# A chunked linear-attention kernel with a gated low-rank layer: decay carried over pairs of chunks, r*k packed into 384 columns, copies shared between ScalarE and VectorE, unread matrix products at the start, and a new hand order

## The chip, the cores and the metric

The kernel runs on one core of a Trainium2 chip. The metric is device time in microseconds for one launch; a time given for "the runs" is the median of several. The profile comes from one further execution. Its engines are called PE (TensorE), DVE (VectorE), ACT (ScalarE), POOL (GpSimd) and SP (SyncE, which here only issues DMAs).

## The reference

Two stages are computed. The first is a linear attention with a decaying state, for batch 4, 8 heads, 768 steps and head dimension 48:

```
for t in range(S):
    cur = einsum('bhd,bhe->bhde', u * k_t, v_t)
    y_t = einsum('bhd,bhde->bhe', r_t, state + cur)
    state = w_t[..., None] * state + einsum('bhd,bhe->bhde', k_t, v_t)
```

The second takes each of the 3072 tokens as a row x of 384 numbers and adds a mixture of low-rank terms: `logits = x @ w_gate` for 8 experts of rank 16, the two largest are kept and normalised by a softmax, and the result is `x + sum_e weight_e * (x @ A[e]) @ B[e]`.

## The kernel before, in words

The 768 steps of a batch are cut into 6 chunks of L = 128 steps, so there are NT = 24 chunks, numbered 0 to 23 across the four batches. A chunk is also one tile of 128 tokens for the second stage. Heads lie in P = 4 pairs; a pair takes 128 partitions, 48 rows for each head and 16 rows of zeros behind them.

Work on chunk t is cut into small stages, each a function of `tile_kernel` with the chunk's number as its argument. A text ORDER (lines 32 to 76) lists all stages of all chunks, and the program issues them exactly so under a manual schedule: an engine's queue is the order in which its stages appear there. Nothing reorders them later, so an instruction that waits holds up everything behind it on its engine.

The stages of the first part, with their engines:
- `load_w`, `load_rk`, `consts` (lines 132 to 160) issue DMAs on SP: w for one or two chunks, r and k of a chunk transposed (512 KB, into a ring of 10 tiles), and the constants u (`ub_f`), A with w_gate (`aw_f`) and B (`b_f`). `load_v` (line 150) issues on POOL's queue: 1, 2 and 3 chunks for the first batch, then all 6 chunks of a batch at once. `castc` (line 162) turns the constants to bf16 on POOL.
- `ln` (ACT) takes log w; `cs` (PE, line 183) sums it over the chunk by a product with a triangle of ones, into `x_ps`; `expp` and `expm` (ACT, lines 189 and 194) give exp of the sums (`ep`, a ring of three tiles) and of their negatives.
- `qmul` (POOL, line 198) is r*k over 512 columns; `rmul` (POOL, line 203) is r times `ep`; `kmul` (DVE, line 208) is k times the negative exponential.
- `dgmm` (PE, line 225) sums r*u*k over each head, by four products, into the bank `kd`; `dv` (DVE, line 238) multiplies v by it. `ktr` (PE, line 218) transposes k into the same bank and `ktev` (ACT, line 230) copies it out as `ks`.
- `amm` (PE, line 244) makes the chunk's scores `a_ps`; `aev` (DVE, line 252) masks them. `kv` (PE, line 258) adds the chunk to the state `s_ps`, which stays in PSUM; `resc` (DVE, line 267) multiplies the state by the chunk's whole decay, after each of the first five chunks of a batch; `sev` (ACT, line 272) copies it out as `sb`.
- `ymd`, `ymS`, `ymv` (PE, lines 277 to 296) add the three parts of y in `y_ps`, and `yev` (ACT, line 298) copies it out as `xT`.

The second part works on gates of three tiles (at the end one of two, and one of one): `zl` (PE, line 309) makes `z_ps`; `top`, `gsel`, `gnorm`, `zw` (DVE), `gexp` (ACT), and `gmul` and `gmul2` (POOL) choose and weigh; `zT` (PE) and `zTev` (DVE, line 378) transpose. Then for each tile `dmm` (PE, line 385), `oev` (ACT, line 394) and `store` (a DMA on SP, line 399).

PSUM is full: `x_ps`, `y_ps`, `kd` and `s_ps` have one buffer each, `a_ps` one of two banks, and `z_ps`, `zT_ps` and `d_ps` share two. So the next chunk's `cs` waits until `kmul` has read `x_ps`, the next `amm` until `aev` has read `a_ps`.

Of the kernel before, what the change touches and what calls it, by code (L numbers as in the profile page):

```python
# [36 lines left out]
ktr.2 ktev.2 cs.4 expp.4 expm.4 ymd.2 load_rk.7 kv.2 resc.2 sev.2 qmul.3 dgmm.3 dv.3 load_v.6 ymS.2 ymv.2
yev.2 rmul.3 amm.3 ktr.3 ktev.3 load_rk.8 kmul.4 cs.5 expp.5 expm.5 aev.3 castc.1 zl.2 top.2 gexp.2 ln.6
kv.3 resc.3 sev.3 gsel.2 ymd.3 ymS.3 qmul.4 dgmm.4 ymv.3 yev.3 rmul.4 amm.4 kmul.5 cs.6 load_w.10 dv.4 ktr.4
ymd.4 ymS.4 gmul.2 gnorm.2 rmul.5 aev.4 ymv.4 load_rk.9 gmul2.2 zw.2 expp.6 expm.6 kmul.6 ktev.4 kv.4 resc.4  # L40
ln.8 load_rk.10 load_rk.11 zT.2 zTev.2 yev.4 sev.4 qmul.5 dgmm.5 dv.5 cs.7 expp.7 expm.7 amm.5 aev.5 kmul.7
castc.2 dmm.0 dmm.1 oev.1 store.1 ymd.5 ymS.5 rmul.6 amm.6 aev.6 ymv.5 cs.8 oev.0 store.0 dmm.2 qmul.6
dgmm.6 dv.6 yev.5 zl.5 top.5 gsel.5 expp.8 expm.8 ktr.6 ktev.6 kmul.8 gexp.5 oev.2 store.2 ymd.6 ymv.6 yev.6
kv.6 resc.6 sev.6 qmul.7 dgmm.7 rmul.7 amm.7 load_w.12 cs.9 expp.9 expm.9 gmul.5 gnorm.5 load_rk.13 dv.7
ktr.7 ymd.7 ktev.7 ymS.7 kv.7 load_rk.12 load_w.14 ln.10 aev.7 ymv.7 yev.7 qmul.8 dgmm.8 gmul2.5 zw.5 zT.5
kmul.9 cs.10 resc.7 sev.7 expp.10 expm.10 rmul.8 amm.8 load_v.12 dv.8 ktr.8 ymd.8 ktev.8 zTev.5 dmm.3 dmm.4
oev.3 oev.4 store.3 ymS.8 kv.8 rmul.9 aev.8 ymv.8 yev.8 kmul.10 resc.8 sev.8 qmul.9 dgmm.9 dv.9 load_rk.14
qmul.10 rmul.10 amm.9 aev.9 cs.11 expp.11 expm.11 rmul.11 zl.8 top.8 gsel.8 ktr.9 ktev.9 kmul.11 gexp.8
gmul.8 ln.12 ymd.9 ymS.9 ymv.9 yev.9 kv.9 resc.9 sev.9 qmul.11 dgmm.10 dv.10 gnorm.8 gmul2.8 amm.10 aev.10
load_w.16 cs.12 expp.12 rmul.12 qmul.12 store.4 ktr.10 ktev.10 load_rk.16 load_rk.15 zw.8 expm.12 kmul.12  # L50
dmm.5 oev.5 store.5 load_rk.17 ln.14 ymd.10 ymS.10 ymv.10 yev.10 kv.10 resc.10 sev.10 zT.8 zTev.8 dgmm.11
dv.11 qmul.13 amm.11 cs.13 expp.13 rmul.13 aev.11 dmm.6 oev.6 store.6 dmm.7 dgmm.12 dv.12 qmul.14 expm.13
kmul.13 oev.7 ymd.11 ymS.11 ymv.11 yev.11 amm.12 aev.12 store.7 ktr.12 ktev.12 load_w.20 cs.14 expp.14
expm.14 rmul.14 zl.11 top.11 dgmm.13 dv.13 kv.12 resc.12 kmul.14 ymd.12 ymv.12 gsel.11 load_w.18 amm.13
aev.13 ktr.13 cs.15 ln.16 yev.12 ymd.13 gexp.11 gmul.11 gnorm.11 ktev.13 dgmm.14 dv.14 sev.12 expp.15
expm.15 dmm.8 oev.8 load_rk.18 ymS.13 ymv.13 yev.13 load_v.18 kv.13 amm.14 ktr.14 ktev.14 gmul2.11 zw.11
zT.11 kmul.15 cs.16 ymd.14 qmul.15 dgmm.15 resc.13 sev.13 expp.16 ymS.14 expm.16 rmul.15 zTev.11 dmm.9
dmm.10 oev.9 oev.10 store.9 aev.14 ymv.14 amm.15 yev.14 kv.14 rmul.16 dv.15 ktr.15 ktev.15 qmul.16 qmul.17
kmul.16 load_rk.19 resc.14 sev.14 cs.17 expp.17 expm.17 aev.15 zl.14 top.14 gexp.14 kv.15 resc.15 gsel.14
gmul.14 dgmm.16 dv.16 qmul.18 kmul.17 ymd.15 ymS.15 ymv.15 gnorm.14 gmul2.14 amm.16 aev.16 ktr.16 ln.18  # L60
cs.18 rmul.17 zw.14 dmm.11 sev.15 yev.15 ymd.16 ktev.16 kv.16 resc.16 load_rk.20 expp.18 expm.18 rmul.18
kmul.18 store.8 dgmm.17 dv.17 qmul.19 ymS.16 ymv.16 oev.11 zT.14 zTev.14 amm.17 aev.17 cs.19 sev.16 store.10
load_w.22 yev.16 ymd.17 ln.20 expp.19 expm.19 rmul.19 dgmm.18 dv.18 qmul.20 dmm.12 kmul.19 dmm.13 oev.13
ymS.17 ymv.17 yev.17 load_rk.21 amm.18 aev.18 ktr.18 ktev.18 cs.20 zl.17 ymd.18 top.17 kv.18 resc.18 gsel.17
expp.20 expm.20 kmul.20 store.11 dgmm.19 dv.19 oev.12 store.12 load_rk.22 gexp.17 gmul.17 gnorm.17 gmul2.17
sev.18 ymv.18 yev.18 amm.19 aev.19 dmm.14 oev.14 store.14 rmul.20 cs.21 expp.21 rmul.21 ktr.19 ktev.19
load_rk.23 ymd.19 ymS.19 ymv.19 kv.19 qmul.21 dgmm.20 qmul.22 zw.17 zT.17 amm.20 expm.21 kmul.21 ln.22 cs.22
yev.19 resc.19 sev.19 dv.20 ktr.20 ymd.20 expp.22 expm.22 rmul.22 zTev.17 dmm.16 aev.20 ymS.20 ymv.20
kmul.22 ktev.20 kv.20 dgmm.21 resc.20 dv.21 oev.16 store.16 amm.21 aev.21 cs.23 yev.20 zl.20 ymd.21 top.20
gsel.20 sev.20 expp.23 expm.23 rmul.23 ktr.21 ktev.21 kmul.23 dmm.15 amm.22 gexp.20 gmul.20 gnorm.20 kv.21  # L70
resc.21 store.13 dgmm.22 ymS.21 oev.15 store.15 dmm.17 oev.17 ymv.21 yev.21 sev.21 gmul2.20 zw.20 zT.20
store.17 dv.22 ktr.22 ymd.22 ktev.22 ymS.22 zTev.20 dmm.19 oev.19 qmul.23 dgmm.23 aev.22 ymv.22 amm.23
yev.22 dv.23 dmm.18 oev.18 store.18 aev.23 zl.22 top.22 gexp.22 gsel.22 kv.22 resc.22 dmm.20 oev.20 store.20
store.19 ymd.23 sev.22 ymS.23 ymv.23 yev.23 gmul.22 gnorm.22 gmul2.22 zw.22 zT.22 zTev.22 dmm.21 dmm.22
oev.21 oev.22 store.21 store.22 zl.23 top.23 gexp.23 gsel.23 gmul.23 gnorm.23 gmul2.23 zw.23 zT.23 zTev.23
dmm.23 oev.23 store.23
# [377 lines left out]
```

## Time and profile before

| what | value |
|---|---|
| median of three runs | 99.08 us (97.99, 99.08, 99.55) |
| the profiled execution | 97.83 us |
| its span, first to last instruction | 96.1 us |
| busy in the span | PE 73.8, DVE 75.6, ACT 72.9, POOL 67.0 us |
| DMA | 25.09 MB moved, mean 261 GB/s |

A row of the table of windows gives a stretch, its length, and then for each engine its busy time and number of instructions, the granted TensorE clock, the share of the 16 DMA engines that was busy, and what they moved. A row of a timeline gives start, length, engine, line, operation and tiles; the bracket gives the idle time ahead of it and what ended it. In a timeline a "x4" merges four instructions that follow each other. The chain of work that ended last is followed back from the last instruction; its rows give start, length and what. A row of the groups gives busy time and mean length of one, then the idle time ahead of them and its causes. Instructions of one engine overlap a little, so the distance between two starts is often less than the length of the first.

### The profile page before, as it was taken

The page shows a single profiled execution, that of the slowest core. Times are in us where ns is not written, and L with a number is a line of the kernel's source. Part 1 is how long each engine was busy: PE and PEld are TensorE (multiplying, and loading weights), DVE is VectorE, ACT ScalarE, POOL GpSimd, SP SyncE. Part 2 cuts the span into 40 slices and gives each one's busy share as a digit, 9 for nine tenths or more (in the row PEclk, how much of TensorE's full clock was granted, in tenths as well). Part 3 has the DMA queues.
Part 4 walks back from the last instruction along what each step waited for, and adds up shares of the span by engine and source line. Part 5 has one row for each costly group of instructions (what it writes and reads, how often), then busy time and mean ns, then how long its engine had stood idle before and what let it go on. Part 6 is the DMA issues. An engine that isn't in the chain of part 4 may idle for free.

```text
span 96.1 us, 3361 instructions
## 1 busy us (share of the span) xinstructions
PE 73.8 (77%) x1312; PEld 56.5 (59%) x1312; DVE 75.6 (79%) x180; ACT 72.9 (76%) x159; POOL 67.0 (70%) x85
## 2 busy tenths in 40 slices
...
GB/s 56 318 243 285 317 412 422 413 419 312 275 412 380 201 24 162 388 322 215 375 422 406 403 409 229 237 291 405 238 51 240 328 159 96 83 67 186 163 1 82
DMA packets 10096, 25.09 MB, mean 261 GB/s; under 512 B 1248, under 2 KB 4960, under 8 KB 10080
## 3 DMA queue, kind: packets, MB, share of 16 engines
...
q8 instruction: 10, 0.16, 0.7%
q14 instruction: 6, 0.05, 0.2%
...
## 4 chain that ended last, share of the span: by engine, by line
DVE 39%; PE 36%; issue 11%; POOL 4%; ACT 4%; DMA 3%; POOLq 0%; ACTq 0%; DVEq 0%
DVE at L254 11%; DVE dv L241 6%; PE z_ps L314 5%; PE y_ps L295 5%; PE kd L223 4%; PE x_ps L186 4%; PE a_ps L249 4%; DVE zw L366 3%; DVE s_ps L270 3%; PE y_ps L280 3%; PE y_ps L289 3%; DMA w_in<-in_w_dram 3%; PE d_ps L391 2%; DVE tp L326 2%; PE kd L228 2%
## 5 line engine op out<-in xcount | busy, mean ns | idle before, releaser
L254 DVE TENSOR_TENSOR at<-a_ps,mask 128x1024 bf16<-128x1024 f32 x24 | 29.1, 1213 | 3.6 <-PE a_ps L249 3.6
L200 POOL TENSOR_TENSOR q<-rk 128x512 bf16<-128x512 f32 x24 | 30.2, 1267 | 0.0
L205 POOL TENSOR_TENSOR rd<-rk,ep 128x512 bf16<-128x512 f32 x24 | 28.1, 1179 | 1.8 <-ACT ep L191 1.6
L191 ACT ACTIVATE ep<-x_ps 128x512 f32<-128x512 f32 x24 | 14.4, 602 | 5.1 <-PE x_ps L186 4.7
L186 PE MATMUL x_ps<-tri,lw 128*128 128x128 f16 x96 | 10.7, 242 | 8.1 <-ACT lw L176 6.9
L300 ACT CAST xT<-y_ps 128x512 bf16<-128x512 f32 x24 | 14.1, 590 | 2.7 <-PE y_ps L295 2.7
L396 ACT COPY res<-d_ps 128x384 f32<-128x384 f32 x24 | 11.3, 490 | 4.6 <-PE d_ps L391 4.1
L196 ACT ACTIVATE x_ps<-x_ps 128x512 f32<-128x512 f32 x24 | 14.4, 601 | 0.0
L241 DVE TENSOR_TENSOR dv<-v_bf,kd 128x384 bf16<-128x384 bf16 x24 | 13.0, 544 | 1.2 <-PE kd L228 1.1
L186 PEld LDWEIGHTS <-lw 128*128 128x128 f16 x96 | 6.7, 107 | 10.4 <-ACT lw L176 7.5
L176 ACT ACTIVATE lw<-w_in 128x768 f16<-128x768 f32 (+1 forms) x13 | 10.3, 793 | 2.7 <-DMA w_in<-in_w_dram 2.7
L347 POOL TENSOR_TENSOR pe<-sel,ge 128x24 f32<-128x24 f32 (+2 forms) x9 | 2.1, 228 | 13.9 <-ACT ge L334 9.5
L295 PE MATMUL y_ps<-at,v_bf 128*48 128x128 bf16 x192 | 10.4, 233 | 1.3 <-DVE at L254 1.1
L235 ACT COPY ks<-kd 128x384 bf16<-128x384 bf16 x20 | 9.6, 482 | 2.0 <-PE kd L223 1.5
L280 PE MATMUL y_ps<-ident,dv 128*128 128x128 bf16 x96 | 10.0, 231 | 0.1
L289 PE MATMUL y_ps<-rd,sb 48*48 48x128 bf16 x160 | 8.5, 229 | 0.7 <-ACT sb L275 0.7
L228 PE MATMUL kd<-ub,q 128*128 128x8 bf16 x96 | 6.1, 169 | 3.9 <-POOL ub L164 3.9
L295 PEld LDWEIGHTS <-v_bf 128*48 128x48 bf16 x192 | 6.7, 107 | 3.4 <-issue 1.6
L391 PE MATMUL d_ps<-b_b,zT 128*128 128x384 bf16 x24 | 7.8, 327 | 0.4 <-DVE zT L381 0.2
L389 PE MATMUL d_ps<-ident,xT 128*128 128x96 bf16 x96 | 8.1, 207 | 0.0
L314 PE MATMUL z_ps<-aw_b,xT 128*128 128x136 bf16 x96 | 7.8, 235 | 0.3 <-ACT res L396 0.3
L270 DVE TENSOR_TENSOR s_ps<-s_ps,ep 128x192 f32<-128x192 f32 x20 | 7.2, 359 | 0.9 <-PE s_ps L264 0.7
...
## 6 DMA issues: line engine op xcount, KB each, us to landing
...
```

The source lines that it names most:

```text
L186: nc.tensor.matmul(x_ps[:, p, :], lhsT=lwof(t, p), rhs=tri, start=True, stop=True)
L191: nc.scalar.activation(out=ep[:, :, 1:L + 1], in_=st[t]["x"], func=ACT.Exp)
L196: nc.scalar.activation(out=x, in_=x, func=ACT.Exp, scale=-1.0)
L200: nc.gpsimd.tensor_mul(q, st[t]["rk"][:, 0], st[t]["rk"][:, 1])
L205: nc.gpsimd.tensor_mul(rd, st[t]["rk"][:, 0], st[t]["ep"][:, :, 0:L])
L241: nc.vector.tensor_mul(o[:, :, 0:D], vseq[t], dg.to_broadcast([128, H, D]))
L254: nc.vector.tensor_mul(at.rearrange("s g p f -> s (g p) f"), st[t]["a_ps"].rearrange("s g p f -> s (g p) f"), mask.to_broadcast([128, H, L]))
L280: nc.tensor.matmul(y_ps[:, p, :], lhsT=st[t]["dv"][:, 2 * p:2 * p + 2, :].rearrange("p a b -> p (a b)"), rhs=ident, start=(p == 0), stop=F ...
L289: nc.tensor.matmul(st[t]["y_ps"][s_, p, :], lhsT=st[t - 1]["sb"][s_, p, :], rhs=st[t]["rd"][s_, p, :], start=False, stop=False, skip_group ...
L295: nc.tensor.matmul(st[t]["y_ps"][g * 64:g * 64 + D, p, :], lhsT=vseq[t][:, h, :], rhs=st[t]["at"][:, g, p, :], start=False, stop=(h >= H - ...
L300: nc.scalar.copy(out=xT, in_=st[t]["y_ps"])
L314: nc.tensor.matmul(z_ps[:, i, :], lhsT=st[t0 + i]["xT"][:, p, :], rhs=aw_b[:, p, :], start=(p == 0), stop=(p == P - 1))
```

## The change

1. **Decay over pairs.** In an odd chunk `cs` also adds the whole sum of the chunk before, by four more products with a tile of ones. `ep` is now two tiles that hold a pair of chunks each, and `resc` runs only after odd chunks (8 times instead of 20).
2. **r*k on 384 columns.** The host puts the 48 rows of the fourth pair's heads, as three pieces of 16, into the zero rows of the other three pairs. `qmul` then reads three pairs, and `dgmm` has three products instead of four.
3. **Unread products.** `warm` issues products of 512 columns of a zero tile into a PSUM tile that nobody reads: 9 at the start, 8 behind `cs.0`, one behind `dgmm.0` and one behind `dgmm.1`.
4. **v** of batches 2 to 4 comes in loads of three chunks (nine loads in all instead of six) into five smaller buffers.
5. **Copies by tile.** Lists say which copies go to DVE: eight `ktev`, one `sev`, three `oev`, two casts of constants and `qmul` of chunk 0. Two `zTev` go to ACT.
6. **The last gate**, of one tile, forms its weights in two fused DVE instructions in place of `gsel`, `gmul`, `gmul2` and `zw`.
7. **A new ORDER** of all stages.

```diff
+Q_ON_DVE = (0,)
+CAST_ON_DVE = (0, 2)
+KT_ON_DVE = (0, 2, 9, 12, 13, 15, 19, 22)
+S_ON_DVE = (14,)
+Y_ON_DVE = ()
+OUT_ON_DVE = (0, 16, 22)
+ZT_ON_ACT = (2, 17)
 ORDER = """
-load_w.0 load_rk.0 load_w.1 load_w.2 load_rk.1 ln.0 consts.0 cs.0 expp.0 load_v.0 load_rk.2 load_v.1
-load_rk.3 expm.0 kmul.0 load_w.4 ln.1 cs.1 expp.1 expm.1 ln.2 load_v.3 rmul.0 amm.0 consts.1 aev.0 load_rk.4
+warm.9 load_rk.1 load_w.0 load_rk.0 qmul.1 load_v.0 load_v.1 ln.0 cs.0 warm.8 load_w.1 expp.0 expm.0 kmul.0
+consts.0 qmul.0 load_w.2 ln.1 cs.1 load_rk.2 load_w.4 castc.0 load_rk.3 rmul.0 amm.0 load_w.8 load_rk.4
+load_v.3 dgmm.0 warm.1 dv.0 ktr.0 ymd.0 consts.1 load_w.6 expp.1 expm.1 rmul.1 kmul.1 qmul.2 ln.2 cs.2
+expp.2 expm.2 rmul.2 ktev.0 kv.0 dgmm.1 warm.1 sev.0 qmul.3 aev.0 ymv.0 amm.1 yev.0 dv.1 ktr.1 kmul.2 cs.3
...
+    def warm(n):
+        if not idle:
+            idle["ps"] = pp.tile([128, 512], F32, name="idle_ps", tag="m", bufs=2)
+        for _ in range(n):
+            nc.tensor.matmul(idle["ps"], lhsT=zero[:, 0:128], rhs=zero, start=True, stop=True)
+
+    def copy(on_dve, o, i):
+        if on_dve:
+            nc.vector.tensor_copy(out=o, in_=i)
+        else:
+            nc.scalar.copy(out=o, in_=i)
...
-        n = {0: 1, 1: 2, 3: 3}[t] if t < NC else NC
-        v_bf = wk.tile([128, NC, H, D], BF16, name="v_bf", bufs=4)
+        n = {0: 1, 1: 2, 3: 3}[t] if t < NC else VL
+        v_bf = wk.tile([128, VL, H, D], BF16, name="v_bf", bufs=VB)
...
-            nc.tensor.matmul(x_ps[:, p, :], lhsT=lwof(t, p), rhs=tri, start=True, stop=True)
+            nc.tensor.matmul(x_ps[:, p, :], lhsT=lwof(t, p), rhs=tri, start=True, stop=t % WL == 0)
+            if t % WL:
+                nc.tensor.matmul(x_ps[:, p, :], lhsT=lwof(t - 1, p), rhs=ones, start=False, stop=True)
...
-        q = wk.tile([128, P, L], BF16, name="q")
-        nc.gpsimd.tensor_mul(q, st[t]["rk"][:, 0], st[t]["rk"][:, 1])
+        q = wk.tile([128, PQ, L], BF16, name="q")
+        (nc.vector if t in Q_ON_DVE else nc.gpsimd).tensor_mul(q, st[t]["rk"][:, 0, 0:PQ], st[t]["rk"][:, 1, 0:PQ])
...
-        for p in range(P):
-            nc.tensor.matmul(dg, lhsT=st[t]["q"][:, p, :], rhs=ub[:, p, :], start=(p == 0), stop=(p == P - 1))
+        for p in range(PQ):
+            nc.tensor.matmul(dg, lhsT=st[t]["q"][:, p, :], rhs=ub[:, p, :], start=(p == 0), stop=(p == PQ - 1))
...
-        nc.scalar.copy(out=ks, in_=kT[:, :, 0:D])
+        copy(t in KT_ON_DVE, ks, kT[:, :, 0:D])
...
-        if t % NC < NC - 1:
+        if t % WL == WL - 1 and t % NC < NC - 1:
             d_ = st[t]["ep"][:, :, L:L + 1]
             nc.vector.tensor_mul(s_ps, s_ps, d_.to_broadcast([128, P, D]))
```

More of the change, by code (lines that the diff above doesn't have):

```diff
@@ L22 @@
 P = H // 2
+PQ = P - 1
 HD = H * D
@@ L37 @@
[L37 to L76, printed above, removed]
+VL = 3
+VB = 5
+Q_ON_DVE = (0,)
+CAST_ON_DVE = (0, 2)
@@ new lines @@
+load_rk.11 expp.9 expm.9 kmul.9 resc.7 load_rk.14 qmul.9 oev.2 store.2 zT.5 zTev.5 cs.10 yev.7 ymd.8
+load_rk.15 aev.8 ktev.8 dgmm.9 dv.9 sev.7 ymS.8 expp.10 expm.10 kmul.10 dmm.3 oev.3 store.3 dmm.4 oev.4
+store.4 kv.8 ymv.8 yev.8 ktr.9 ktev.9 ln.12 rmul.9 amm.9 aev.9 cs.11 qmul.10 dgmm.10 dv.10 zl.8 top.8 ymd.9
+sev.8 kv.9 ymS.9 resc.9 expp.11 expm.11 gexp.8 ktr.10 ktev.10 load_w.16 load_v.12 ymv.9 yev.9 rmul.10 amm.10
+qmul.12 qmul.11 dgmm.11 sev.9 load_rk.16 gsel.8 gmul.8 rmul.11 load_w.18 kmul.11 cs.12 expp.12 expm.12
@@ new lines @@
+gmul.11 gnorm.11 gmul2.11 ymd.13 ymS.13 kv.13 qmul.16 dv.14 ktr.14 ktev.14 store.8 rmul.14 aev.13 ymv.13
+yev.13 zw.11 zT.11 rmul.15 ln.20 resc.13 sev.13 kmul.15 zTev.11 dgmm.15 dv.15 qmul.17 amm.14 aev.14 ymd.14
+cs.16 expp.16 expm.16 rmul.16 load_rk.21 ln.18 store.7 dmm.10 ktr.15 ktev.15 load_rk.19 load_v.18 kv.14
+ymS.14 dmm.9 ymv.14 yev.14 dgmm.16 qmul.18 oev.10 store.10 sev.14 kv.15 kmul.16 resc.15 sev.15 amm.15
+load_rk.20 cs.17 expp.17 expm.17 rmul.17 ymd.15 zl.14 dv.16 ktr.16 ktev.16 aev.15 top.14 load_w.22 gexp.14
```

95 lines of the change are left out of this document (75 added, 20 removed).

## The prediction

> **What bounds the kernel now.** I read the table of windows first, then the chain of work that ended last, then the timeline of the first 26 us by engine.
>
> ```profile
> core 0: us, PE busy (x) PEld busy (x) DVE busy (x) ACT busy (x) POOL busy (x), PEclk, DMA share, GB/s
> 4.00:8.00 4.00, 0.90 (x8) 0.52 (x6) 0.69 (x1) 1.61 (x3) 2.40 (x2) 1.00 0.99 257
> ...
> 12.00:25.26 13.26, 12.49 (x166) 9.94 (x167) 8.58 (x14) 9.44 (x19) 10.81 (x11) 1.00 1.04 384
> 25.26:85.50 60.24, 56.00 (x1094) 43.46 (x1095) 58.91 (x139) 55.30 (x124) 49.74 (x55) 1.00 0.76 264
> ```
>
> From 25.26 to 85.50 us DVE is busy 58.91 of 60.24 us: it is the bound, 1.3 us from full. ACT (55.3) and PE (56.0) are close behind. Before that stretch DVE is not the bound: from 12.00 to 25.26 it is busy 8.58 of 13.26 us while PE is busy 12.49. So a gain has to come from less DVE work in the long stretch, or from the 25 us ahead of it and the 11 us behind it.
>
> ```profile
> DVE 39%; PE 36%; issue 11%; POOL 4%; ACT 4%; DMA 3%; POOLq 0%; ACTq 0%; DVEq 0%
> ...
> 7.56 4.73 issue
> ...
> 23.86 1.37 PE z_ps L314 x12
> ...
> 51.30 0.72 PE z_ps L314 x12
> ```
>
> The same twelve products take 1.37 us at 23.86 and 0.72 us at 51.30. The granted clock in the windows reads 1.00 in both places, so that column does not show it; the durations do. PE runs the first chunks at about half pace, although it is nearly always busy there.
>
> ```profile
> 0.74 0.38 SPq L141 DMA_DIRECT2D w_in<-in_w_dram  x1
> 1.74 0.74 POOL L154 DMA_DIRECT2D v_bf<-in_v_dram  x1
> 3.26 0.52 ACT L176 ACTIVATE lw<-w_in 128x384 f16<-128x384 f32 x1 [1.25 <-DMA w_in<-in_w_dram]
> 5.60 0.69 DVE L210 TENSOR_TENSOR kd__141<-rk,x_ps 128x512 bf16<-128x512 f32 x1 [2.01 <-ACT x_ps L196]
> 8.81 1.22 DVE L254 TENSOR_TENSOR at<-a_ps,mask 128x1024 bf16<-128x1024 f32 x1 [2.52 <-PE a_ps L249]
> 11.08 0.69 DVE L210 TENSOR_TENSOR kd__180<-rk,x_ps 128x512 bf16<-128x512 f32 x1 [1.04 <-DMA rk<-in_rk_dram]
> 12.31 0.21 POOL L164 CAST ub<-ub_f 128x32 bf16<-128x32 f32 x1 [4.75 <-DMA ub_f<-in_ublk_dram]
> 12.57 0.25 PE L228 MATMUL kd<-ub,q 128*128 128x8 bf16 x4 [3.87 <-POOL ub L164]
> 12.86 0.55 DVE L241 TENSOR_TENSOR dv<-v_bf,kd 128x384 bf16<-128x384 bf16 x1 [1.09 <-PE kd L228]
> 25.26 0.32 DVE L326 MAX8 tp<-z_ps 128x8 f32<-128x8 f32 x3 [1.09 <-PE z_ps L314]
> ...
> v_bf<-in_v_dram POOLq DMA_DIRECT2D x1, 96.0 KB, 6.4
> ub_f<-in_ublk_dram SPq DMA_DIRECT2D x1, 16.0 KB, 9.2
> ```
>
> So the ramp has two parts: until 12.3 us it waits for DMA (POOL 4.75 us for the little ub_f, which lands 9.2 us after its issue and is the 4.73 us of "issue" in the chain), and from there to 25.26 us it is PE at half pace.
>
> **The long stretch, by pitches.** Busy times of DVE overlap, so I price its work by the distance between starts.
>
> ```profile
> 28.99 0.68 DVE L210 TENSOR_TENSOR kd__537<-rk,x_ps 128x512 bf16<-128x512 f32 x1
> 29.59 0.36 DVE L270 TENSOR_TENSOR s_ps<-s_ps,ep 128x192 f32<-128x192 f32 x1
> 29.86 0.35 DVE L381 COPY zT<-zT_ps 128x384 bf16<-128x384 bf16 x1
> 30.12 0.54 DVE L241 TENSOR_TENSOR dv<-v_bf,kd 128x384 bf16<-128x384 bf16 x1
> 30.58 1.22 DVE L254 TENSOR_TENSOR at<-a_ps,mask 128x1024 bf16<-128x1024 f32 x1
> 31.72 0.68 DVE L210 TENSOR_TENSOR kd__589<-rk,x_ps 128x512 bf16<-128x512 f32 x1
> ...
> L270 DVE TENSOR_TENSOR s_ps<-s_ps,ep 128x192 f32<-128x192 f32 x20 | 7.2, 359 | 0.9 <-PE s_ps L264 0.7
> L396 ACT COPY res<-d_ps 128x384 f32<-128x384 f32 x24 | 11.3, 490 | 4.6 <-PE d_ps L391 4.1
> L235 ACT COPY ks<-kd 128x384 bf16<-128x384 bf16 x20 | 9.6, 482 | 2.0 <-PE kd L223 1.5
> L200 POOL TENSOR_TENSOR q<-rk 128x512 bf16<-128x512 f32 x24 | 30.2, 1267 | 0.0
> L154 POOL DMA_DIRECT2D v_bf<-in_v_dram x6 | 3.6, 601 | 0.2 <-issue 0.2
> ```
>
> The pitches: kmul 0.60, resc 0.27, the copy zT 0.26, dv 0.46, the masking aev 1.14.
> - resc runs at the end of each pair of chunks only, 8 times instead of 20. In this stretch that takes 9 away (16 to 7): 9 x 0.27 = 2.4 us less.
> - Copies come to DVE. Six of the eight ks copies lie here; the nearest row is the zT copy, the same 384 bf16 out of PSUM: 6 x 0.26 = 1.6 us (with dv's 0.46 as the upper end, 2.8). Two result copies of 384 f32 (tiles 0, 16) by dv's 0.46: 0.9 (lower end 2 x 0.26). One sb copy of 192 f32: at most resc's 0.27. The cast of b_b, between 0.26 and 0.46: 0.3. Two zT copies leave: 0.5 less.
> - Sum on DVE: -2.4 + 1.6 + 0.9 + 0.3 + 0.3 - 0.5 = +0.2 us. dv of the last chunk moves behind the last aev, 0.46 from this stretch into the tail, with no net effect.
>
> So the bound of the long stretch is not moved. Other engines are relieved: ACT by 8 x 0.48 + 3 x 0.49 and more, some 5 us; POOL by 24 x 1.27 x 0.25 = 7.6 us (q at 384 of 512 columns, taken in proportion; the low end is nothing) plus one q and two casts, against three more v loads at 0.60 = 1.8 us. All of this lies beside DVE and I count it as nothing; its cover is DVE's 58.9 us, and if DVE had been shorter these would have been next. The deeper ep tiles (two pairs instead of three singles) hold four chunks and let nothing wait. SP's new order keeps the ring of ten r,k tiles, and the DMA share of 0.76 in this stretch leaves room.
>
> PE is the engine that gets more.
>
> ```profile
> 39.38 0.38 PE L223 MATMUL kd<-ident,kd__694 128*128 128x128 bf16 x4
> 39.60 0.39 PE L280 MATMUL y_ps<-ident,dv 128*128 128x128 bf16 x4
> ...
> 41.36 0.26 PE L228 MATMUL kd<-ub,q 128*128 128x8 bf16 x4
> 41.55 0.40 PE L249 MATMUL a_ps<-rd,kd__819 48*128 48x128 bf16 x8
> ```
>
> Four 128x128 products take 0.22 us, four dgmm products 0.19. Each odd chunk now adds four "ones" products to cs: 12 x 0.22 = 2.6 us in all. Each dgmm loses one of four: 24 x 0.05 = 1.2. In the long stretch about +1.1 us on 56.0 of 60.2: PE goes to about 95%. It stays under DVE, but the odd chunks' loop kmul, cs, expp, expm, kmul is 0.22 longer. For such collisions of two nearly full engines I add 0.5 us (bounds 0, if all stays hidden, and 2.6, if every added product is exposed).
>
> **The ramp.** r,k of chunk 1 is now loaded first, then w.0, r,k of chunk 0, w.1, then ub. Before, w.0 alone (0.20 MB) was there 2.5 us after its issue at 0.74. With 0.52 MB ahead of it at the 257 GB/s of 4 to 8 us, that becomes about 2.0 us later: ln.0 at 5.2 instead of 3.26, and kmul.0, as far behind it as before, at about 7.5 instead of 5.60. On POOL the issue of v.0 and v.1 now stands behind q.1, which waits for r,k of chunk 1: landing at 4.2 to 5.2, q.1 0.95 (three quarters of 1.27), so v.0 is issued at about 5.8 instead of 1.74. Before, it took 6.4 us to land in the full queue; that gives 12.2 us. The lower bound is w.0's 2.5 us, that is 8.3. dv.0 waits for it in DVE's queue, and behind dv.0 stand kmul.1, ktev.0 and aev.0, and with them amm.1 and the whole of chunk 1. ub, now issued ahead of w.2, should come sooner than 12.3. So dv.0 is at about 12.2 instead of 12.86: the wait for ub_f goes and v.0 is late next. aev.0 and kmul.1, before at 8.81 and 11.08, come after it. The start itself loses; the gain must come behind it.
>
> From dv.0 to the point that before reached at 25.26 (dv, aev of chunks 0 to 3, kmul 1 to 4, one resc, two ks copies) DVE has 4 x 0.46 + 4 x 1.14 + 4 x 0.60 + 0.27 + 2 x 0.26 = 9.6 us of work. If PE runs at full pace, as the 17 unread products of 512 columns ahead of chunk 0 are there to see to, DVE is the bound from here: 12.2 + 9.6 = 21.8, and 0.2 us of waits make it 22.0. That is 3.3 us before 25.26.
>
> The Trainium skill, "TensorE: Matmul & The Clock Gate", Part 1, states that PE starts at half clock, is released after one sustained busy window of some 3.4 us, and falls back after an idle window as long; it puts the whole warm-up at under 1% of a usual span. This trace disagrees on the size: z_ps is still slow at 23.86 us. By that 1% the change would win about 1 us here in place of 3.3, an estimate from that page.
>
> **The tail.** For the last tile, pe moves from POOL to DVE and g goes away into zw.
>
> ```profile
> 90.21 0.21 ACT L334 ACTIVATE ge<-df 128x8 f32<-128x8 f32 x1 [0.57 <-DVE sel L340]
> ...
> 90.74 0.16 DVE L353 TENSOR_REDUCE den<-pe 128x1 f32<-128x8 f32 x1 [0.54 <-POOL pe L347]
> 90.93 0.16 DVE L354 RECIPROCAL den<-den 128x1 f32<-128x1 f32 x1
> 91.47 0.29 DVE L366 TENSOR_TENSOR zw<-z_ps,g 128x128 bf16<-128x128 f32 x1 [0.38 <-POOL g L360]
> ```
>
> From reciprocal to zw 0.54 becomes the 0.19 from sum to reciprocal: -0.35; from ge to the sum, 0.53, about -0.1. Together -0.45 us.
>
> **The sum.** Span 96.1 - 3.3 (ramp) - 0.45 (tail) + 0.2 (DVE) + 0.5 (PE) = 93.1 us. Around the span lie 97.83 - 96.1 = 1.7 us: 94.8 for that execution, 3.0 less. The profiled execution is the quickest of the four known (97.83, 97.99, 99.08, 99.55; mean 98.6, median of the three runs 99.08). 98.6 - 3.0 = 95.6; I take 95.4, as the relieved ACT and POOL can only help.
>
> **The rivals.**
> 1. PE falls back to half pace. Between the unread products and ymd.0, which waits for dv.0, PE has little to do; before, PE's 3.87 us pause ahead of 12.57 led into 12 slow microseconds. Then PE is the bound again until zl.2. It starts about a microsecond ahead and pays four ones products in each of two chunks at the slow pace (0.43 us each): about 0.3 us gained, with the tail 0.8: 97.8. For it: PE was nearly full from 12 us and stayed slow, so that dense products, not mere occupation, seem to be needed. Against: the unread products are dense. The page's idle window speaks for this rival too.
> 2. Slower: copies stall DVE. DVE takes its instructions in order, and 11 ks and result copies wait on PE there. On ACT such waits cost 2.0 us over 20 and 4.6 over 24. At those means DVE loses 8 x 0.10 + 3 x 0.19 = 1.4 us; the plan must place them well to lose nothing. At 0.7 us a copy, what stands behind each wait (kmul, aev, and with them PE) costs 7.7 us: 103. It decides from 0.3 us each, where the 3.0 us gain is gone; from about 0.5 us it is slower by 2%.
> 3. v.0 and ub land early, near the lower bound: dv.0 by 9.5, other waits of the start (expm, amm) then leading, 2 us more gained: 93.4.
>
> **How the numbers follow.** Forecast (94 to 97) 0.50; rival 3 or better 0.17; rival 1 0.18; rival 2 0.15. The range leaves out the far half of rival 3 and most of rival 2: 92.4 to 98.6. About 2% is what a measurement of this kernel can tell from no change. Faster by over 2% (below 97.1): 0.50 + 0.17 and a little of rival 1, 0.70; the same: most of rival 1 and the mild part of rival 2, 0.18; slower: 0.12.
>
> **What would show it.** Ramp right: z_ps of the first gate takes about 0.7 us in place of 1.37, the first tp starts near 22 us, dv.0 near 12 and waits for v's DMA. Long stretch: DVE's busy share stays at 97% or more from the first tp to the last aev, s_ps x8 and ks x8 on DVE. Tail: zw follows the reciprocal within 0.2 us. Wrong, if z_ps of the first gate is slow, if DVE's idle time ahead of ks, res or kd passes 3 us, or if PE passes DVE in the long stretch.

## The result, and the profile after

| | before | after |
|---|---|---|
| median of six executions each | 98.80 us (97.99 to 99.55) | 103.15 us (102.03 to 104.54) |
| ratio, with its 95% interval | | 1.041 (1.032 to 1.049) |
| the profiled execution, and its span | 97.83, 96.1 us | 102.25, 100.5 us |

The change makes the kernel slower by 4%; 95.4 us (92.4 to 98.6) was predicted. Executions of one kernel spread by up to 6 us here, so below each median covers all executions of its kernel, while a ratio with its interval compares the undisturbed ones alone and is the one to go by where the two differ.

The place of the loss is found by laying the starts of the masking (`aev`, `at<-a_ps,mask` on DVE), of which each chunk has one, side by side, with the first `tp` (on DVE too), where the long stretch of the prediction begins:

| start of | before | after | difference | added since the row above |
|---|---|---|---|---|
| aev.3 | 22.94 | 22.82 | -0.12 | -0.12 |
| first tp | 25.26 | 24.56 | -0.70 | -0.58 |
| aev.16 | 63.32 | 63.21 | -0.11 | +0.59 |
| aev.17 | 66.48 | 70.55 | +4.07 | +4.18 |
| aev.18 | 68.67 | 73.95 | +5.28 | +1.21 |
| aev.23 | 84.28 | 87.89 | +3.61 | -1.67 |
| end of the span | 96.1 | 100.5 | +4.4 | +0.79 |

So the ramp gave 0.1 us at aev.3 and 0.7 us at the first `tp`. The forty microseconds up to aev.16 cost nothing counted from aev.3, and 0.6 us counted from the first `tp`. One single step lost 4.2 us, the next chunk another 1.2 that had come back by aev.23, and the tail lost 0.8 (of which 0.49 is `dv.23`, moved there from the stretch above). The first view is the table of windows of after, cut at its own first `tp` and its last `aev`; the columns are those of the first fence of the prediction.

```profile
core 0: us, PE busy (x) PEld busy (x) DVE busy (x) ACT busy (x) POOL busy (x), PEclk, DMA share, GB/s
4.00:8.00 4.00, 3.54 (x15) 1.28 (x13) 0.53 (x2) 1.70 (x4) 2.92 (x5) 1.00 0.96 322
12.00:24.56 12.56, 10.72 (x168) 8.58 (x168) 10.54 (x17) 8.41 (x17) 6.58 (x7) 0.73 1.05 373
24.56:89.10 64.54, 57.18 (x1099) 44.68 (x1097) 57.99 (x136) 53.45 (x119) 46.26 (x57) 0.97 0.78 244
```

In the long stretch DVE's busy time fell by 0.9 us to 57.99, but the stretch is 4.3 us longer (64.54 for 60.24). DVE went from 98% busy to 90%: it waits. The granted clock of 0.73 in the ramp says that PE is at half pace for a part of it. What is waited for stands on the page of after: the chain of work that ended last, two groups, and the row of the DMA issues.

```profile
DVE 31%; DMA 29%; PE 16%; issue 11%; POOL 7%; ACT 2%; POOLq 0%; SPq 0%; DVEq 0%; ACTq 0%
...
L235 POOL TENSOR_TENSOR q<-rk 128x384 bf16<-128x384 f32 x23 | 22.9, 997 | 8.4 <-DMA rk<-in_rk_dram 6.9
L276 DVE TENSOR_TENSOR dv<-v_bf,kd 128x384 bf16<-128x384 bf16 x24 | 13.1, 544 | 8.6 <-DMA v_bf<-in_v_dram 7.3
...
v_bf<-in_v_dram POOLq DMA_DIRECT2D x7, 288.0 KB, 8.1
```

DMA, 3% of the chain before, is 29% of it now. DVE is idle 7.3 us ahead of `dv` for v: 3.49 us at the start, 0.19 us for chunk 12 and 3.57 us for chunk 18. The long pieces of the chain of after show the three loads (start, length, what):

```profile
1.80 2.43 issue
4.28 0.99 POOL q L235
5.46 7.12 DMA v_bf<-in_v_dram
...
23.79 0.74 PE z_ps L349 x12
...
39.83 8.39 DMA v_bf<-in_v_dram
...
54.21 5.00 DMA rk<-in_rk_dram
59.34 0.66 POOL q L235
60.30 1.13 POOL rd L240
61.43 8.29 DMA v_bf<-in_v_dram
```

The first is at the start, where the prediction expected it. The last, from 54.21 on, it did not expect. The timeline of after by engine shows these two, and the tail:

```profile
7.48 0.69 DVE L245 TENSOR_TENSOR kd__158<-rk,x_ps 128x512 bf16<-128x512 f32 x1 [3.48 <-DMA rk<-in_rk_dram]
8.08 1.03 DVE L235 TENSOR_TENSOR q<-rk 128x384 bf16<-128x384 f32 x1
12.71 0.55 DVE L276 TENSOR_TENSOR dv<-v_bf,kd 128x384 bf16<-128x384 bf16 x1 [3.49 <-DMA v_bf<-in_v_dram]
13.31 0.58 PE L258 MATMUL kd<-ident,kd__158 128*128 128x128 bf16 x4 [3.48 <-DVE dv L276]
16.68 0.61 PE L258 MATMUL kd<-ident,kd__218 128*128 128x128 bf16 x4
19.85 0.40 PE L258 MATMUL kd<-ident,kd__277 128*128 128x128 bf16 x4
24.56 0.32 DVE L361 MAX8 tp<-z_ps 128x8 f32<-128x8 f32 x3
...
59.34 1.00 POOL L235 TENSOR_TENSOR q<-rk 128x384 bf16<-128x384 f32 x1 [1.32 <-DMA rk<-in_rk_dram]
60.30 1.19 POOL L240 TENSOR_TENSOR rd<-rk,ep 128x512 bf16<-128x512 f32 x1
61.43 0.59 POOL L186 DMA_DIRECT2D v_bf<-in_v_dram  x1
69.81 0.55 DVE L276 TENSOR_TENSOR dv<-v_bf,kd 128x384 bf16<-128x384 bf16 x1 [3.57 <-DMA v_bf<-in_v_dram]
...
90.89 0.17 DVE L395 TENSOR_REDUCE den<-pe 128x2 f32<-128x16 f32 x1 [0.84 <-POOL pe L389]
...
95.42 0.16 DVE L396 RECIPROCAL den<-den 128x1 f32<-128x1 f32 x1
95.62 0.35 DVE L411 SCALAR_TENSOR_TENSOR zw<-z_ps,den,pe 128x128 bf16<-128x128 f32 x1
```

And the timeline of before, for the load of v that serves the same chunk 18:

```profile
54.59 0.59 POOL L154 DMA_DIRECT2D v_bf<-in_v_dram  x1 [0.21 <-issue]
...
67.61 0.54 DVE L241 TENSOR_TENSOR dv<-v_bf,kd 128x384 bf16<-128x384 bf16 x1
```

Before, POOL issues this load 13.0 us ahead of `dv.18`, which waits for nothing. After, it is issued at 61.43, behind `q.17`, which waits for r,k of chunk 17, which SP issued at 54.21, behind a store. DVE is ready for `dv.18` at 66.24, 4.8 us after the issue; the load lands 8.29 us after it, and 3.57 us are lost. PE pauses with it (3.56 us ahead of the transposes at 70.42) and comes back slowly: the granted clock is 0.83 in 68 to 72 us and 0.74 in 72 to 76. I take the loss of 4.2 us to be this wait and what follows from it; the experiments test that.

### The profile page after: what moved, and what is told of

The parts are those of the page before. It is cut to its first block, busy times and chain, and to the rows that moved or that the text cites. A ratio compares the mean times of both kernels' runs of the same rounds, so it can differ in the third digit from the quotient of the medians.

```text
span 100.5 us, 3411 instructions
## 1 busy us (share of the span) xinstructions
PE 79.8 (79%) x1354; PEld 59.0 (59%) x1355; DVE 77.2 (77%) x182; ACT 69.7 (69%) x149; POOL 60.8 (60%) x83
## 4 chain that ended last, share of the span: by engine, by line
DVE 31%; DMA 29%; PE 16%; issue 11%; POOL 7%; ACT 2%; POOLq 0%; SPq 0%; DVEq 0%; ACTq 0%
DMA v_bf<-in_v_dram 24%; DVE at L289 11%; DVE dv L276 5%; DMA rk<-in_rk_dram 5%; POOL rd L240 3%; POOL q L235 3%; PE y_ps L330 3%; PE kd L258 3%; PE a_ps L284 2%; PE z_ps L349 2%; DVE ks L160 2%; DVE zw L418 2%; ACT res L162 1%; DVE tp L361 1%; PE d_ps L443 1%
## 5 line engine op out<-in xcount | busy, mean ns | idle before, releaser
L235 POOL TENSOR_TENSOR q<-rk 128x384 bf16<-128x384 f32 x23 | 22.9, 997 | 8.4 <-DMA rk<-in_rk_dram 6.9
L218 PE MATMUL x_ps<-tri,lw 128*128 128x128 f16 x96 | 12.3, 233 | 1.4 <-ACT lw L208 0.8
L162 ACT COPY res<-d_ps 128x384 f32<-128x384 f32 x21 | 9.9, 483 | 3.5 <-PE d_ps L443 3.3
L218 PEld LDWEIGHTS <-lw 128*128 128x128 f16 x96 | 8.0, 104 | 4.5 <-ACT lw L208 2.3
L162 ACT COPY ks<-kd 128x384 bf16<-128x384 bf16 x12 | 5.8, 480 | 5.3 <-PE kd L258 5.0
L389 POOL TENSOR_TENSOR pe<-sel,ge 128x24 f32<-128x24 f32 (+1 forms) x8 | 1.9, 231 | 10.9 <-ACT ge L369 3.8
L443 PE MATMUL d_ps<-b_b,zT 128*128 128x384 bf16 x24 | 8.4, 350 | 0.0
L349 PE MATMUL z_ps<-aw_b,xT 128*128 128x136 bf16 x96 | 7.1, 222 | 0.3 <-ACT res L162 0.3
L156 PE MATMUL idle_ps<-zero 128*128 128x512 bf16 x18 | 6.3, 507 | 1.2 <-DVE zero L101 1.2
L315 PEld LDWEIGHTS <-dv 128*128 128x128 bf16 x96 | 6.7, 102 | 0.8 <-issue 0.4
## 6 DMA issues: line engine op xcount, KB each, us to landing
aw_f<-in_aw_dram SPq DMA_DIRECT2D x1, 272.0 KB, 10.4
```

The lines of the kernel that those rows point to most:

```text
L162: nc.scalar.copy(out=o, in_=i)
L218: nc.tensor.matmul(x_ps[:, p, :], lhsT=lwof(t, p), rhs=tri, start=True, stop=t % WL == 0)
L235: (nc.vector if t in Q_ON_DVE else nc.gpsimd).tensor_mul(q, st[t]["rk"][:, 0, 0:PQ], st[t]["rk"][:, 1, 0:PQ])
L315: nc.tensor.matmul(y_ps[:, p, :], lhsT=st[t]["dv"][:, 2 * p:2 * p + 2, :].rearrange("p a b -> p (a b)"), rhs=ident, start=(p == 0), stop=F ...
L443: nc.tensor.matmul(d_ps, lhsT=st[t]["zT"], rhs=b_b, start=False, stop=True, skip_group_check=True)
```

## The experiments

The theory (A, where an expectation uses a letter): the main loss is the late issue of v of chunk 18, some 4 us; beside it, and separate from it, the ramp's missing gain is the PE pause ahead of `dv.0` (rival 1 of the prediction), about 2 us. Against it stand three others: the copies on DVE and the new order cost the time all over, and the wait for v only collects slack that would be lost elsewhere; the late v.0 at the start delays everything behind it; and the unread products or the r*k on 384 columns matter by themselves. All times are medians; since the executions spread, I compare each kernel's distance to the kernel before on the same chip. For after that distance is +4.35 us, and its ratio 1.041. Where no ratio is given, the executions were too few for one. In kernels with one line less in ORDER, line numbers are one lower than in after.

**v of chunk 18 earlier (v18_early), v of chunk 0 earlier (v0_first), both (v0_v18).** ORDER alone changes, here cut to the neighbours:

```diff
-expm.13 load_v.15 dv.12
+expm.13 load_v.15 load_v.18 dv.12
...
-load_rk.19 load_v.18 kv.14
+load_rk.19 kv.14
```

> The changed kernel with one entry of ORDER moved: load_v.18 stands right behind load_v.15 instead of some 14 us later. Theory A (v of chunk 18 is issued too late on POOL's queue, at 61.43 us for a dv that is due at 66.2): DVE's 3.57 us wait ahead of dv.18 goes, PE does not fall to half pace behind it, and the time is about 4.5 us less than the changed kernel's, 98.6 us. Rival B (the DMA engines are full there, so whichever transfer is moved ahead makes r,k of chunks 18 to 20 late instead): the wait moves to POOL's q or to kmul, and the time is 101.5 us or more. Rival C (the slower start and the added PE work are what costs): 102 us or more.

```diff
-load_rk.0 qmul.1 load_v.0 load_v.1 ln.0
+load_rk.0 load_v.0 load_v.1 qmul.1 ln.0
```

> The changed kernel with qmul.1 moved behind the issue of v.0 and v.1 on POOL. Theory A (dv.0 waits until 12.7 us for v.0, whose issue waits behind q.1, and PE goes back to half pace in that 3.5 us pause): v.0 is issued at about 1.7 us, dv.0 runs before 10.5 us, PE stays at full pace from 8 us on, and the ramp is 2 to 3 us shorter; the late v.18 stays, so about 100.5 us. Rival (r,k of chunks 0 and 1 and w.1 land later, since v takes its share of the DMA engines, so that dv.0 is no sooner): 103 us, no change.

> Both moves together. If the two losses are separate and both are what theory A says: 103.2 - 4.5 - 2.5 = about 96 us, below the kernel before (98.8). If the long stretch lost for other reasons (PE at 95%, copies on DVE): 98.5 us or more.

v18_early: 99.61 us (98.88 to 100.02) against 98.09, a distance of +1.5, so 2.8 better than after; ratio 1.027 (1.019 to 1.035). The timeline of v18_early:

```profile
46.44 1.12 POOL L185 DMA_DIRECT2D v_bf<-in_v_dram  x2
66.91 0.55 DVE L275 TENSOR_TENSOR dv<-v_bf,kd 128x384 bf16<-128x384 bf16 x1
67.70 1.21 DVE L288 TENSOR_TENSOR at<-a_ps,mask 128x1024 bf16<-128x1024 f32 x1
```

With the issue some 20 us ahead (the second of the two loads in the first row), `dv.18` waits for nothing and `aev.17` starts at 67.70 instead of 70.55. The span is 97.1 us instead of 100.5: the time is not lost again elsewhere, so the wait does not merely collect slack, and the theory holds for the main loss. Its size stays rough: 2.8 us by the distances, 2.85 at aev.17, but by the ratios only 1.4 of 4.1 points, with intervals that just overlap.

v0_first: 100.82 us (97.61 to 102.69), a distance of +2.7: 1.6 better than after. `load_v.0` is issued at 1.74, `dv.0` runs at 10.87 and the first `tp` at 22.19, 2.4 earlier than in after, while `dv.18` still waits 3.8 us. So by the trace the late v.0 has a part in the slow ramp. Four executions this far apart do not show how large it is beside the late v of chunk 18.

v0_v18: 96.85 us (96.12 to 101.91), a distance of -1.2; ratio 1.009 (1.001 to 1.017). The median lies below the kernel before and the ratio above 1. By either, the two moves together win back most of the loss (after: 1.041), and this version is not faster than the kernel before.

**Two mirrors on the kernel before.** before_v18late puts its load of v for chunk 18 as late as after has it; before_q384 takes over only the r*k on 384 columns.

```diff
-yev.13 load_v.18 kv.13
+yev.13 kv.13
...
-gsel.14 gmul.14 dgmm.16
+gsel.14 gmul.14 load_v.18 dgmm.16
```

> The kernel before with one entry moved: load_v.18 stands behind gmul.14, so that POOL issues it at about 62.4 us instead of 54.6, some 5 us ahead of dv.18 (67.6 us). Theory A (the place of this one load is the loss, in either kernel): it lands some 8.5 to 9 us later, at about 71, DVE waits about 3.3 us for it and PE turns slow behind that: 3.5 to 5 us slower than before, about 102.5 us. Rival (the late load hurts only with the loads of three chunks and the other order): within 1.5 us of before.

It took 103.37 us (101.90 to 104.75) against 98.33: +5.0; ratio 1.067 (1.034 to 1.100). The timeline of before_v18late:

```profile
61.53 0.59 POOL L153 DMA_DIRECT2D v_bf<-in_v_dram  x1 [0.20 <-PE a_ps L248]
...
70.49 0.55 DVE L240 TENSOR_TENSOR dv<-v_bf,kd 128x384 bf16<-128x384 bf16 x1 [3.58 <-DMA v_bf<-in_v_dram]
```

This one move, in a kernel with nothing else changed, makes the same wait (3.58 for 3.57 us) and costs as much as the whole change did. That is the strongest evidence for the theory.

```diff
-        q = wk.tile([128, P, L], BF16, name="q")
-        nc.gpsimd.tensor_mul(q, st[t]["rk"][:, 0], st[t]["rk"][:, 1])
+        q = wk.tile([128, PQ, L], BF16, name="q")
+        nc.gpsimd.tensor_mul(q, st[t]["rk"][:, 0, 0:PQ], st[t]["rk"][:, 1, 0:PQ])
...
-        for p in range(P):
-            nc.tensor.matmul(dg, lhsT=st[t]["q"][:, p, :], rhs=ub[:, p, :], start=(p == 0), stop=(p == P - 1))
+        for p in range(PQ):
+            nc.tensor.matmul(dg, lhsT=st[t]["q"][:, p, :], rhs=ub[:, p, :], start=(p == 0), stop=(p == PQ - 1))
```

> The kernel before with r*k on 384 columns and three dgmm products alone. POOL has about 6.5 us less work. By the prediction (POOL lies beside DVE's full stretch): no change, within 1 us. Rival (POOL's q decides when dgmm, dv and the transposes come): 2 us faster.

It took 98.66 us (97.08 to 99.08) against 98.16: no gain, though q went from 1267 to 999 ns and POOL has 6.5 us less to do. No execution comes down to the 96.2 us of the rival; POOL does not bound this kernel.

**The unread products.** no_warm takes every `warm` out of after's ORDER; pause_filled has twelve products behind `dgmm.0` in place of one; before_filled adds to the kernel before nothing but unread products (and their zero tile).

```diff
-dgmm.0 warm.1 dv.0
+dgmm.0 warm.12 dv.0
```

```diff
-load_w.0 load_rk.0 load_w.1 load_w.2 load_rk.1 ln.0 consts.0 cs.0 expp.0
+warm.6 load_w.0 load_rk.0 load_w.1 load_w.2 load_rk.1 ln.0 consts.0 cs.0 warm.12 expp.0
...
-rmul.0 amm.0 consts.1
+rmul.0 amm.0 warm.18 consts.1
```

> The changed kernel without any unread product (they feed no output). If the products free PE's pace for the start only and the pause at 9.8 to 13.3 us undoes it: within 1 us of the changed kernel, 103 us, and PE turns fast later than 19.4 us. If they are what brought PE to full pace at 19.4 us in place of 24.9: 1.5 to 3 us slower, 105 us. If they only delay cs.0 and the first chunk: 102.5 us.

> The changed kernel with 12 unread products behind dgmm.0 instead of one, which fill PE's pause from about 9.5 to 12.1 us while dv.0 waits for v.0. Theory (an idle pause of some 3.5 us puts PE back to half pace): PE stays at full pace from 8 us on, the transposes behind dv.0 take about 0.38 us in place of 0.58, the first tp starts 1 to 2 us sooner, and the time is 101 to 102 us. Rival (unread zero products do not hold the pace, or the slow stretch from 13 us has another cause): the transposes take 0.58 us and the time is 103 us.

> The kernel before with unread products alone: 6 at the start, 12 behind cs.0, 18 behind amm.0, where PE waited 3.87 us for ub (they feed no output). Nothing else is changed. By the prediction's ramp term (PE at full pace behind the first dv makes DVE the bound, 3.3 us): the transposes of chunks 0 to 3 take 0.38 us in place of 0.58 to 0.61, the first tp starts at about 22.5 in place of 25.3, and the time is 2.5 to 3.3 us below the kernel before. Rival (the first chunks wait for DMA and ACT anyway): less than 1 us.

no_warm: 102.79 us (101.28 to 104.40) against 98.09, a distance of +4.7: not to be told from after. As the change places them, the products do nothing for the time that these runs could tell. The timeline of no_warm has the same half pace, for as long:

```profile
12.85 0.59 PE L257 MATMUL kd<-ident,kd__140 128*128 128x128 bf16 x4 [2.29 <-DVE dv L275]
16.12 0.61 PE L257 MATMUL kd<-ident,kd__199 128*128 128x128 bf16 x4
19.50 0.42 PE L257 MATMUL kd<-ident,kd__257 128*128 128x128 bf16 x4
```

pause_filled: 101.47 us (98.06 to 101.95) against 98.33, a distance of +3.1: 1.2 better than after by the medians, and no ratio. Its timeline:

```profile
9.67 2.75 PE L155 MATMUL idle_ps<-zero 128*128 128x512 bf16 x11
13.00 0.38 PE L257 MATMUL kd<-ident,kd__158 128*128 128x128 bf16 x4 [0.58 <-DVE dv L275]
22.79 0.32 DVE L360 MAX8 tp<-z_ps 128x8 f32<-128x8 f32 x3
```

The transposes take 0.38 us at once (0.58 in after), though `dv.0` waits for v as in after (12.39 for 12.71), and the first `tp` comes 1.8 us earlier. It was the pause, not the late v alone, that kept the ramp slow.

before_filled: 95.18 us (94.83 to 98.11) against 98.16: 3.0 us faster by the medians, but only 1.1% by the ratio, 0.989 (0.979 to 0.9996). It has the lowest median of all. Its timeline:

```profile
9.27 4.06 PE L139 MATMUL idle_ps<-zero 128*128 128x512 bf16 x17
14.66 0.38 PE L232 MATMUL kd<-ident,kd__162 128*128 128x128 bf16 x4 [0.39 <-DVE dv L250]
23.48 0.32 DVE L335 MAX8 tp<-z_ps 128x8 f32<-128x8 f32 x3
```

Although `dv.0` runs only at 14.05 (12.86 before), the first `tp` is at 23.48 instead of 25.26: from `dv.0` on, the ramp takes 9.4 us in place of 12.4. Not all of that is owed to the products. before_v18late has the same start and before_q384 nearly the same, both without any unread product; in their traces `dv.0` runs at 14.23 and 14.36 and the first `tp` comes 9.9 us behind it, at 24.16 and 24.30, with the first group of transposes still at 0.59 us. So beside these three traces holding the pace is worth 0.7 to 1.8 us at the first `tp`, which does not explain 3.0 us.

**Both repairs together (v18_filled):** after, with `load_v.18` as in v18_early and `warm.12` as in pause_filled.

> The changed kernel with the two single repairs: load_v.18 right behind load_v.15, and 12 unread products behind dgmm.0 in place of one. If the late v.18 (3.5 us) and the pause (1.7 us) are separate losses and all of the loss: 103.2 - 5.2 = 98 us, level with the kernel before. If they overlap: 99.5 us.

98.37 us (97.48 to 99.36) against 98.16: a distance of +0.2; ratio 1.021 (1.003 to 1.039). The two repairs alone gave 2.8 and 1.2; together they give 4.1 of 4.35. By the distances, then, the two losses are separate and nearly the whole of what the change lost. By the ratios (1.041 for after, 1.021 here) only half of it is won back, with wide intervals. The repairs bring the kernel level with before by the medians and leave it 2% slower by the ratio; they do not bring it ahead.

**The other half of the start.** start_tile_order is v0_v18 with the start's loads in tile order, and tile_order_filled has in addition w.2 ahead of r,k of chunk 1 and nine more unread products behind `ymd.0`.

```diff
-load_rk.1 load_w.0 load_rk.0 load_v.0 load_v.1 qmul.1 ln.0
+load_w.0 load_rk.0 load_v.0 load_v.1 ln.0
...
-consts.0 qmul.0
+consts.0 load_rk.1 qmul.0
...
-load_v.3 dgmm.0
+load_v.3 qmul.1 dgmm.0
```

```diff
-consts.0 load_rk.1 qmul.0 load_w.2 ln.1
+consts.0 load_w.2 load_rk.1 qmul.0 ln.1
...
-dv.0 ktr.0 ymd.0 consts.1
+dv.0 ktr.0 ymd.0 warm.9 consts.1
```

> The run with both moves (v.0 first, v.18 early) with the start in tile order as well: w.0, r,k of chunk 0, w.1, ub, r,k of chunk 1, and q.1 behind rmul.0 on POOL. Theory (r,k of chunk 1 ahead of everything delays ln.0 and kmul.0 by 2 us, and PE then pauses): kmul.0 at 5.6 us in place of 7.5 and dv.0 by 9.5 us: 1 to 2 us less than with both moves alone, about 95.3 us. Rival (amm.1 and dv.1 wait for r,k of chunk 1 and q.1 then, so the end of the start is the same): 96.9 us.

> The run that starts in tile order, with w.2 loaded ahead of r,k of chunk 1 and 9 more unread products behind ymd.0, where PE paused for 2.4 us until ln.2 had its w. Theory (the pause puts PE to half pace, and w.2 is what ends it): PE stays at full pace from 5 us on, the first tp starts at about 21 us in place of 22.7, and the time is about 95.5 us, 1.5 less than with the tile order alone and 2.5 to 3 below the kernel before. Rival (r,k of chunk 1 is now late in w.2's place): 97 us.

start_tile_order: 97.15 us (95.18 to 101.27) against 98.33, a distance of -1.2, ratio 0.992 (0.980 to 1.003). By the median it is level with v0_v18 and nearer to the rival's number than to mine; by the ratio it is 1.7 points below v0_v18 and nearer to mine. These runs do not settle it. `dv.0` runs at 8.35, 2.5 us earlier than in v0_first, yet the first `tp` comes at 22.70. The timeline of start_tile_order shows why:

```profile
8.96 0.38 PE L257 MATMUL kd<-ident,kd__155 128*128 128x128 bf16 x4 [0.41 <-DVE dv L275]
11.93 0.61 PE L217 MATMUL x_ps<-tri,lw 128*128 128x128 f16 x4 [2.37 <-ACT lw L207]
14.48 0.61 PE L257 MATMUL kd<-ident,kd__218 128*128 128x128 bf16 x4
```

PE was at full pace at 8.96, waited 2.37 us for w of chunk 2, and was at half pace again behind it.

tile_order_filled: 97.83 us (97.32 to 98.64) against 98.16, ratio 1.019 (1.008 to 1.029): no gain, where 2.5 to 3 us were expected. The timeline of tile_order_filled:

```profile
13.17 0.40 PE L258 MATMUL kd<-ident,kd__227 128*128 128x128 bf16 x4
21.63 0.32 DVE L361 MAX8 tp<-z_ps 128x8 f32<-128x8 f32 x3 [0.32 <-PE z_ps L349]
30.19 0.56 DVE L276 TENSOR_TENSOR dv<-v_bf,kd 128x384 bf16<-128x384 bf16 x1 [2.64 <-DMA v_bf<-in_v_dram]
...
76.35 0.40 PE L284 MATMUL a_ps<-rd,kd__1972 48*128 48x128 bf16 x8 [1.66 <-POOL rd L240]
77.47 1.57 PE L349 MATMUL z_ps<-aw_b,xT 128*128 128x136 bf16 x12
```

PE keeps its pace through the ramp and the first `tp` is the earliest of all, but at 30.19 DVE waits 2.64 us for the next load of v, issued at 21.75, and aev.6 starts no earlier than in start_tile_order (31.26 for 31.05). By aev.16 the lead is there again (61.29 for 62.21). It is lost for good between aev.20 and aev.23, which takes 11.3 us in place of 8.2: POOL's q of chunk 22 waits 2.53 us for its r,k, PE waits 1.66 us for the `rd` behind it, and then PE is at half pace (twelve `z_ps` products in 1.57 us, with a granted clock of 0.50 from 78 to 80 us). It is the loss of chunk 18 once more, with other loads, in other places.

**All copies back on ACT (copies_act),** on v0_v18:

```diff
-KT_ON_DVE = (0, 2, 9, 12, 13, 15, 19, 22)
-S_ON_DVE = (14,)
+KT_ON_DVE = ()
+S_ON_DVE = ()
...
-OUT_ON_DVE = (0, 16, 22)
-ZT_ON_ACT = (2, 17)
+OUT_ON_DVE = ()
+ZT_ON_ACT = ()
```

> The run with both moves, with every copy back on its old engine (ks, sb and res on ACT, zT on DVE). By rival 2 of the prediction (copies stall DVE's queue) it is faster than with both moves alone, by up to 3 us, 94 us. By the sum of DVE's pitches DVE has about 2.9 us less and ACT about 5 us more work: ACT becomes the fuller engine (75 us), and in an order that was planned for the shared copies the time is the same or up to 2 us more, 97 to 99 us.

101.84 us (101.40 to 102.93) against 98.33, ratio 1.059 (1.044 to 1.075): 4.7 worse than v0_v18 by the distances, 5.0 points by the ratios. The groups of DVE in copies_act, and then in after (idle time ahead behind the last bar):

```profile
L275 DVE TENSOR_TENSOR dv<-v_bf,kd 128x384 bf16<-128x384 bf16 x24 | 13.1, 544 | 4.5 <-PE kd L262 4.5
```

```profile
L160 DVE COPY ks<-kd 128x384 bf16<-128x384 bf16 x8 | 2.8, 350 | 0.1
L160 DVE COPY res<-d_ps 128x384 f32<-128x384 f32 x3 | 1.7, 552 | 0.9 <-PE d_ps L443 0.9
```

In after, DVE waits 0.1 us ahead of its eight ks copies and 0.9 ahead of three result copies. Taking them away costs far more: DVE loses 4.5 us ahead of `dv` (1.4 in v0_v18). I read this as ACT emptying the bank `kd` later, so that the next `dgmm` waits for it; but only 1.6 us of the waits ahead of `dgmm` name ACT's copies, so that reading is shown in part only. In this ORDER the copies belong on DVE; rival 2 of the prediction falls, and with it the copies as a cause. I had expected 97 to 99 us, and had not priced that the copies hold up `kd`.

## Why the prediction was wrong, by its steps

1. **What bounds the kernel:** right. DVE is full wherever nothing is late, and before_q384 shows that POOL's relief is worth nothing (q measured at 997 ns, 950 estimated).
2. **DVE's sum of +0.2 us and the +0.5 for the fuller PE:** not contradicted. From aev.3 to aev.16 it is 40.39 us after and 40.38 before; from the first `tp`, where the prediction's stretch begins, 38.65 and 38.06. The two orders differ in what stands ahead of these marks (`dv.4` stands ahead of the first `tp` in after and behind it in before), so terms as small as these cannot be told apart.
3. **The step that failed: "three more v loads at 0.60 = 1.8 us. All of this lies beside DVE and I count it as nothing".** A load's issue time is not its price. A load costs nothing as long as the distance from its issue to its use exceeds its landing time. Before, that distance for chunk 18 was 13.0 us; the new ORDER makes it 4.8; landing takes 8.3. The danger could have been seen ahead of the run: in the new ORDER the load stands behind `qmul.17`, which waits for r,k of chunk 17, and the prediction itself shows 6.4 us to landing for a load a third as large. It also took the DMA share of 0.76, a mean over the stretch, as room; while this load was under way (61.43 to 69.72) the share was 1.00. The step is the +4.18 in the table of starts; v18_early and before_v18late show it from both sides.
4. **The ramp, "If PE runs at full pace ... DVE is the bound from here: 12.2 + 9.6 = 21.8":** the times up to `dv.0` came out (kmul.0 7.48 for 7.5, dv.0 12.71 for 12.2, waiting for v.0 as said). The condition failed, and this is the second step that failed. PE, at full pace at 8.5 us (the products of `cs.1` start 55 ns apart), paused 3.48 us for `dv.0`, and its transposes took 0.58 and 0.61 us until 17.3 (0.40 at 19.85). That is rival 1, given 0.18. The ramp's gain is 0.12 us at aev.3 and 0.70 at the first `tp`, the place that the forecast names, instead of 3.3. The term itself was near: pause_filled shows 10.4 us from `dv.0` to `tp`, and before_filled 9.4, where 9.8 was forecast and after took 11.9 (before_v18late and before_q384, where PE was slow at first, took 9.9).
   The Trainium skill, "TensorE: Matmul & The Clock Gate", Part 1, says that PE falls back after an idle window of about 3.4 us. Here 3.48 us agree, but 2.37 us (start_tile_order) and 1.66 us (tile_order_filled, at 76.35) sufficed as well, and 2.46 us (tile_order_filled, at 30.80) did not. The rule of the Trainium skill there, that the warm-up is under 1%, is neither borne out nor refuted: before_filled, which holds the pace through the ramp, is 1.1% faster by the ratio, with an interval from 0.04 to 2.1%.
5. **What would show it** was misread in one point: `z_ps` of the first gate takes 0.74 us, as forecast for a ramp that is right. PE was fast again by then; the slow part lay ahead of it.
6. **The tail, -0.45:** the fused weights gave -0.34 (zw 0.20 behind the reciprocal, 0.54 before), but the wait for POOL's `pe` of the gate ahead went from 0.23 to 0.84 (90.89), and the last `d_ps` from 0.35 to 0.51 us as PE was slow there. With `dv.23` counted where it was before, the tail is 0.3 longer.
7. **Rival 2** fell (copies_act), and **rival 3** (v.0 early) is what v0_first does: it moved dv.0 to 10.87, not to 9.5.

The sum: 3.2 us from the ramp, 3.5 from the long stretch (4.2 lost there, less the 0.7 that was forecast) and 0.75 in the tail make 7.45, and the distance between the span forecast, 93.1, and 100.5 is 7.4. Counted from the first `tp` instead of aev.3, the ramp's part is 2.6 and the stretch's 4.1.

What stays open in part: why v18_filled is no faster than before. At aev.3 it is at 20.77 us (before 22.94) and at aev.16 at 61.27 (63.32); from there to the end it takes 34.4 us where before took 32.8. One piece can be read in the timeline of v18_filled:

```profile
74.31 1.00 POOL L234 TENSOR_TENSOR q<-rk 128x384 bf16<-128x384 f32 x1 [2.44 <-DMA rk<-in_rk_dram]
76.50 0.40 PE L283 MATMUL a_ps<-rd,kd__1974 48*128 48x128 bf16 x8 [1.57 <-POOL rd L239]
```

POOL's q of chunk 22 waits 2.44 us for r,k, which SP issued at 67.37 behind two stores, and the scores of chunk 21 wait 1.57 us for the `rd` that stands behind it on POOL. From aev.20 to aev.23 this kernel takes 9.6 us, after and start_tile_order 8.2. The traced execution of v0_v18, its slowest (101.91 us), has the same two waits with 3.24 and 2.38 us, and takes 12.0. So another load comes too late as soon as the work ahead of it is faster. The rest, with PE at half pace in the tail of v18_filled, no run took apart.
